# Linear attention into a rational feed-forward layer on one core: weights built with 16-bit low bits, their low parts made by a transfer that adds

## The chip, the cores and the metric

The kernel runs on one core of one Trainium2 chip. The metric is the device time of one execution in microseconds (us); lower is better. Shown are the median of three runs and one profiled execution. The engines are TensorE (PE in the profile, PEld its weight loads), VectorE (DVE), ScalarE (ACT), GpSimd (POOL) and the queue that issues most transfers (SP).

## The reference, cut to what matters

```
kv  = einsum('bhsd,bhse->bhde', k, v)        # 8 batches, 8 heads, 576 positions, 64 wide
out = einsum('bhsd,bhde->bhse', q, kv)
out = out / sqrt(mean(out*out, -1) + 1e-6) * g_norm
x   = out.transpose(0, 2, 1, 3).reshape(4608, 512)
h   = x @ w_in                               # w_in 512 x 2048, 64-bit floats
P   = a0 + a1*h + a2*h^2 + a3*h^3
Q   = 1 + |b0|*|h| + |b1|*h^2
y   = (P / (Q + 1e-6)) @ w_out               # w_out 2048 x 512, 64-bit floats
```

The two weight matrices come as 64-bit floats. The kernel makes 32-bit floats of them on the chip.

## The kernel before, in words

**Tiles and slots.** The 4608 tokens are nine tiles `t` of 512. The 2048 hidden columns are sixteen chunks `c` of 128. A pair `(t, c)` is a slot; slots have a running number `i`, so 0 to 15 are the first tile (t = 0), 16 to 31 the second (t = 1), and so on. One Python loop over the slots sets the order of work on each engine, which is kept as written. In slot `i`, TensorE computes `gemm2` of slot `i-2` (h's function times `w_out`, added up in four `acc` tiles of PSUM), then matmuls of attention for the tile after this one, then `gemm1` of slot `i+1` (x times `w_in` into one of two `h` tiles). ScalarE and VectorE compute the rational function of slot `i` between them (`ew_a`, `ew_b`, `ew_c`: ACT lines L458, L459, L461, L471, L472, DVE lines L460, L462, L468, L476, L478, L484).

**Split and unsplit.** The first tile multiplies 32-bit floats as they are (lines L444 and L507; the profile counts two MATMUL records for each). The other tiles write each operand as a high part rounded to `float32r` and a low part, the difference, and multiply low by high, high by low and high by high: three matmuls (L448 to L450, L511 to L513). The function's result is split in `ew_d` (`gh` on ACT L494, `gl` on DVE L495). `unsplit(t, c)` says where `gemm2` uses whole floats: the first tile, and the last four chunks of the second (`LATE = 12`), because the low parts of those weights are made later.

**Weights.** A unit is a pair of chunks of `w_in` ("wi") or `w_out` ("wo"), 128 x 1024 words of 64 bits; there are sixteen. `fetch_w` loads one through SP. To make 32-bit floats, `signs` (GpSimd, L224) multiplies the high words by zero, which leaves their signs; `conv_a` (ACT, L192, two passes) scales the low and the high words in place; `conv_c` (DVE, for each half of a unit) shifts the high words by 3 and ors them into the signs (L229), then adds the low words (L230). The first two units go another way (`conv_b1`, L208; `conv_b2`, L212 and L216), ahead of the loop. The table `schedule` gives for each unit the slot of its load, of its `conv_a`, and of its split. `signs` of a unit starts, by a dependency added by hand, after DVE's L460 of the slot whose ACT does `conv_a`.

**Splitting weights.** `split_w` casts the unit to its high part on ACT (L247) and, at the end of the slot's DVE work, subtracts on DVE (L254, 128 x 1024). Low parts go where an earlier unit's whole floats stood. The last unit is copied away first (`w_last`).

Of the kernel before, what the change touches and what calls it, by code (L numbers as in the profile page):

```python
# [23 lines left out]
def linear_attention_then_rational_ffn(  # L24
# [93 lines left out]
    def f32(t):  # L118
# [6 lines left out]
        ("wi", 0): (None, None, 13),  # L125
        ("wi", 2): (None, None, 15),
        ("wo", 0): (None, None, 16),
        ("wi", 4): (-1, 0, 17),
        ("wo", 2): (-1, 1, 18),
        ("wi", 6): (-1, 2, 19),  # L130
        ("wo", 4): (-1, 3, 19),
        ("wi", 8): (0, 4, 20),
        ("wo", 6): (0, 5, 21),
        ("wi", 10): (1, 6, 21),
        ("wo", 8): (2, 7, 23),
        ("wi", 12): (3, 8, 23),
        ("wo", 10): (4, 9, 24),
        ("wi", 14): (5, 10, 26),
        ("wo", 12): (6, 11, 33),
# [83 lines left out]
    def signs(u, part):  # L223
        return POOL.tensor_scalar(room(u)[:, part], f32(words(u, part)[1]), 0.0, None, ALU.mult)  # L224

    def conv_c(u, part):
        low, high = words(u, part)
        w = ups[u].bitcast(I32)[:, part]
        DVE.scalar_tensor_tensor(w, high, 3, w, ALU.logical_shift_left, ALU.bitwise_or)  # L229
        DVE.tensor_tensor(w, w, low, ALU.add)  # L230
# [6 lines left out]
    def split_w(u):  # L237
# [11 lines left out]
        def rest():  # L249
# [4 lines left out]
            DVE.tensor_tensor(wl, w, f32(wh), ALU.subtract)  # L254
# [376 lines left out]
    conv_b1(u1, two)  # L631

# [4 lines left out]
    for i, (t, c) in enumerate(slots[:-1]):  # L637
        q_made = ew_a(t, c, ph)
        for u in at_slot(1, i):

            tc.add_manual_dep(signs(u, both).ins, q_made.ins.name, beside, reason="signs beside h")
        if i:
            ew_d(*slots[i - 1])
        rest = {0: [], 1: [], 2: []}
        convs = [lambda u=u, j=j: (conv_b2 if u == u1 else conv_c)(u, (one, two)[j]) for u, j in made.get(i, [])]
# [27 lines left out]
        if c == NF - 2 and t < NTILE - 1:  # L673
# [51 lines left out]
```

## Time and profile before

| | |
|---|---|
| median of 3 runs | 906.61 us (906.58 to 906.76) |
| profiled execution, span from first to last instruction | 904.8 us |
| between that span and the median | 1.8 us |
| PE busy | 895.7 us, 99% |
| DVE busy | 792.6 us, 88% |
| ACT busy | 689.8 us, 76% |
| POOL busy | 50.5 us, 6% |
| DMA, mean over the span | 73 GB/s |

The page gives no time for the profiled execution other than its span, so the sum below is made against 904.8 us and carried over to the median. A busy PE is not a PE at its peak: the matmuls' ends are modelled, and a start-to-start distance says more than a duration. Rows of the timeline give the start in us, the duration in us, engine, line, operation and tiles; in square brackets the idle time ahead of it and what ended that. Rows of windows give the stretch, its length, and for each engine the busy time and the number of instructions, then the granted clock, the share of DMA and GB/s.

### The profile page before, as it was taken

What the parts mean: (1) busy time and instruction counts of PE and PEld (TensorE: products, weight loads), DVE (VectorE), ACT (ScalarE), POOL (GpSimd) and SP (SyncE); (2) the same over time, 40 slices, a digit from 0 to 9 for tenths busy, and PEclk for the clock granted to TensorE, in tenths of its full rate; (3) what the DMA queues carried; (4) which work ended last, traced back from release to release, by engine and by line L of the source; (5) the groups of instructions that cost most, each with busy time, mean ns of one, the idle gap of its engine ahead of it and who ended that gap; (6) DMA issues with size and microseconds to landing.
All of it is one profiled execution on the core that took longest, in us unless ns stands there. A gap on an engine that the chain in (4) does not pass through costs nothing.

```text
span 904.8 us, 11685 instructions
## 1 busy us (share of the span) xinstructions
PE 895.7 (99%) x4278; PEld 676.7 (75%) x4278; DVE 792.6 (88%) x1250; ACT 689.8 (76%) x1167; POOL 50.5 (6%) x63
## 2 busy tenths in 40 slices
PE   8999999999999999999999999999999999999998
PEld 6444446778678788878887888788878887888886
DVE  3998999999897898889887998799778988898887
ACT  5898867888687778777877686778777787777665
POOL 3444310000000000000000000000000000000000
PEclk9999999999999999999999999999999999999999
DMA  9964002211122203210311122121301020201001
GB/s 367 359 239 146 25 24 96 75 42 47 42 91 79 48 1 129 82 35 14 119 58 35 48 88 82 41 49 41 117 24 48 0 70 13 48 0 47 1 1 47
DMA packets 23961, 65.89 MB, mean 73 GB/s; under 512 B 2336, under 2 KB 2336, under 8 KB 23904
## 3 DMA queue, kind: packets, MB, share of 16 engines
q1 hardware_dynamic: 23328, 64.10, 21.6%
q10 hardware_dynamic: 576, 1.05, 0.3%
q8 instruction: 33, 0.54, 0.3%
q14 instruction: 24, 0.20, 0.1%
HBM read 55.58 MB, written 9.57 MB: 72 GB/s over the span
## 4 chain that ended last, share of the span: by engine, by line
PE 88%; DVE 7%; ACT 2%; DMA 1%; issue 1%; SPq 0%; DVEq 0%; ACTq 0%
PE h L448 13%; PE acc L511 12%; PE h L450 12%; PE h L449 12%; PE acc L513 12%; PE acc L512 12%; PE acc L507 5%; PE h L444 4%; PE kvp L331 2%; DMA first<-in_first_dram 1%; DVE q L460 1%; PE ms L375 1%; PE op L362 1%; PE op L363 1%; DVE u L462 1%
## 5 line engine op out<-in xcount | busy, mean ns | idle before, releaser
L448 PE MATMUL h<-x,parts 128*128 128x512 f32 (+1 forms) x516 | 205.7, 399 | 0.0
L450 PE MATMUL h<-x,parts 128*128 128x512 f32 (+1 forms) x516 | 200.5, 389 | 0.0
L458 ACT ACTIVATE d<-h 128x512 f32<-128x512 f32 x143 | 85.8, 600 | 149.2 <-PE h L450 145.8
L512 PE MATMUL acc<-wol,gh 128*128 128x512 f32 x492 | 191.5, 389 | 0.0
L460 DVE SCALAR_TENSOR_TENSOR q<-d,b1abs,q 128x512 f32<-128x512 f32 x143 | 107.1, 749 | 81.1 <-ACT q L459 80.9
L449 PE MATMUL h<-x,wil 128*128 128x512 f32 (+1 forms) x452 | 175.5, 388 | 0.0
L511 PE MATMUL acc<-parts,gl 128*128 128x512 f32 x440 | 171.9, 391 | 0.7 <-ACT ob L519 0.4
L513 PE MATMUL acc<-parts,gh 128*128 128x512 f32 x440 | 171.2, 389 | 0.0
L471 ACT ACTIVATE d<-q,bias 128x512 f32<-128x512 f32 x143 | 105.5, 738 | 28.5 <-DVE q L460 27.5
L448 PEld LDWEIGHTS h<-x,parts 128*128 128x128 f32 x516 | 96.9, 188 | 26.4 <-DVE gl L495 5.0
L461 ACT ACTIVATE u<-h,na 128x512 f32<-128x512 f32 x143 | 112.7, 788 | 0.0
L450 PEld LDWEIGHTS h<-x,parts 128*128 128x128 f32 x516 | 96.9, 188 | 20.6
L472 ACT ACTIVATE d<-d,bias 128x512 f32<-128x512 f32 x143 | 103.6, 724 | 4.7
L478 DVE SCALAR_TENSOR_TENSOR u<-u,na,d 128x512 f32<-128x512 f32 x143 | 106.8, 747 | 0.0
L468 DVE SCALAR_TENSOR_TENSOR u<-u,na,h 128x512 f32<-128x512 f32 x143 | 106.0, 741 | 0.7
L512 PEld LDWEIGHTS acc<-wol,gh 128*128 128x128 f32 x492 | 92.4, 188 | 18.9
L476 DVE SCALAR_TENSOR_TENSOR q<-q,d 128x512 f32<-128x512 f32 x143 | 98.3, 687 | 0.8 <-ACT d L472 0.8
L462 DVE TENSOR_TENSOR u<-u,h 128x512 f32<-128x512 f32 x143 | 97.9, 685 | 0.8
L459 ACT ACTIVATE q<-h,abg 128x512 f32<-128x512 f32 x143 | 98.1, 686 | 0.0
L511 PEld LDWEIGHTS acc<-parts,gl 128*128 128x128 f32 x440 | 82.6, 188 | 19.7 <-DVE gl L495 1.9
L449 PEld LDWEIGHTS h<-x,wil 128*128 128x128 f32 x452 | 85.0, 188 | 16.2 <-issue 0.2
L513 PEld LDWEIGHTS acc<-parts,gh 128*128 128x128 f32 x440 | 82.6, 188 | 17.3
(142 smaller groups left out, 1120.3 us busy)
## 6 DMA issues: line engine op xcount, KB each, us to landing
kvm<-in_kv_dram SPq DMA_DIRECT2D x28, 640.0 KB
raw_wo<-in_w_out_dram SPq DMA_DIRECT2D x8, 1024.0 KB
qr<-in_qT_dram SPq DMA_DIRECT2D x32, 256.0 KB
out_dram<-ob SPq DMA_DIRECT2D x16, 512.0 KB
rb<-rd SPq DMA_DIRECT2D x28, 256.0 KB
raw_wi<-in_w_in_dram SPq DMA_DIRECT2D x6, 1024.0 KB
first<-in_first_dram SPq DMA_DIRECT2D x4, 640.0 KB
raw_wi<-in_w_in_dram SPq DMA_DIRECT2D x4, 512.0 KB
```

Source lines behind the costliest of these rows:

```text
L448: PE.matmul(ph, wh, xl, start=(kc == 0), stop=False)
L449: PE.matmul(ph, wl, xh, start=False, stop=False)
L450: PE.matmul(ph, wh, xh, start=False, stop=(kc == NPAIR - 1))
L460: q_made = DVE.scalar_tensor_tensor(q, d, b1abs, q, ALU.mult, ALU.add)
L461: ACT.activation(u, ph, AF.Identity, bias=na[:, 2:3], scale=na[:, 3:4])
L462: DVE.tensor_tensor(u, u, ph, ALU.mult)
L468: DVE.scalar_tensor_tensor(u, u, na[:, 1:2], ph, ALU.add, ALU.mult)
L471: ACT.activation(d, q, AF.Ln, bias=bias[:, 2:3], scale=QSC)
L478: DVE.scalar_tensor_tensor(u, u, na[:, 0:1], d, ALU.add, ALU.mult)
L511: PE.matmul(o, gl[:, ss], wh, start=(c == 0), stop=False)
L512: PE.matmul(o, gh[:, ss], wl, start=False, stop=False)
L513: PE.matmul(o, gh[:, ss], wh, start=False, stop=(c == NF - 1))
```

## The change

Four edits go together; lines from L222 on move by up to 10 in the new file (L460 becomes L464, L254's place becomes L257 and L258).

1. **Low bits as 16-bit words.** `conv_a` scales the high words first, then writes the scaled low words as 16-bit integers straight into the low half of the words that `signs` wrote. `conv_shift` (DVE, once for a unit, 128 x 1024) shifts the high words in place. `conv_c` is then one addition for each half. `signs` of a unit comes one slot earlier; those of the first two such units stand ahead of the loop, without the dependency on L460.
2. **Low parts by transfer.** In `split_w`, GpSimd writes the negated high part into the low part's place (L257) and then issues a transfer that adds the unit to it (L258). DVE no longer subtracts.
3. **Second tile split throughout.** `unsplit` holds for the first tile alone.
4. **Earlier splits.** The third column of `schedule` runs from slot 11 to 30; it ran from 13 to 35.

```diff
-        ("wi", 0): (None, None, 13),
+        ("wi", 0): (None, None, 11),
...
-        ("wo", 14): (7, 12, 35),
+        ("wo", 14): (7, 12, 30),
     }
-    LATE = 12
...
     def unsplit(t, c):
-        return t == 0 or t == 1 and c >= LATE
+        return t == 0
...
     def conv_a(u, part=both, engine="S"):
         low, high = words(u, part)
-        scale(engine, low, low.bitcast(U32), 2.0**-29)
         scale(engine, f32(high), f32(high), 2.0**-112)
+        to = low if u in units[:2] else ups[u].bitcast(U16).rearrange("p (f w) -> p f w", w=2)[:, part, 0]
+        scale(engine, to, low.bitcast(U32), 2.0**-29)
...
+    def conv_shift(u):
+        high = words(u, both)[1]
+        DVE.tensor_scalar(high, high, 3, None, ALU.logical_shift_left)
+
     def conv_c(u, part):
-        low, high = words(u, part)
         w = ups[u].bitcast(I32)[:, part]
-        DVE.scalar_tensor_tensor(w, high, 3, w, ALU.logical_shift_left, ALU.bitwise_or)
-        DVE.tensor_tensor(w, w, low, ALU.add)
+        DVE.tensor_tensor(w, w, words(u, part)[1], ALU.add)
...
-            DVE.tensor_tensor(wl, w, f32(wh), ALU.subtract)
+            POOL.tensor_scalar(wl, f32(wh), -1.0, None, ALU.mult)
+            POOL.dma_start(wl, w, accum_op=ALU.add)
...
-    signs(u2, both)
+    signs(u2)
     conv_a(u1, one)
     conv_a(u1, two)
+    for u in at_slot(1, 0):
+        signs(u)
     conv_a(u2)
...
     conv_b1(u1, two)
+    conv_shift(u2)
...
-        for u in at_slot(1, i):
-            tc.add_manual_dep(signs(u, both).ins, q_made.ins.name, beside, reason="signs beside h")
+        for u in at_slot(1, i + 1):
+            tc.add_manual_dep(signs(u).ins, q_made.ins.name, beside, reason="signs beside h")
...
         for u in at_slot(1, i):
             conv_a(u)
+            shifts.append(u)
...
+        rest[2] += [lambda u=u: conv_shift(u) for u in shifts]
```

How the order of instructions moves, at two places. In these rows `wow_297` is the unit wo 0 (the third made), `raw_wi_245` the raw words of wi 4 (the fourth), `wiw_317` and `wiw_319` the unit wi 2. The first place is the start, on GpSimd, from the last of its setup on; before:

```order
L115 MEMSET kvh_130 128x128
L116 MEMSET kvl_136 128x128
L224 TENSOR_SCALAR wow_297<-raw_wo_155 128x1024 [waits DMAHW4_49]
L224 TENSOR_SCALAR wiw_335<-raw_wi_245 128x1024 [waits DMAHW5_49,DVE_49]
L224 TENSOR_SCALAR wow_367<-raw_wo_251 128x1024 [waits DMAHW0_49,DVE_49]
```

and in the changed kernel:

```order
L116 MEMSET kvh_130 128x128
L117 MEMSET kvl_136 128x128
L225 TENSOR_SCALAR wow_297<-raw_wo_155 128x1024 [waits DMAHW4_49]
L225 TENSOR_SCALAR wiw_303<-raw_wi_245 128x1024 [waits DMAHW5_49]
L225 TENSOR_SCALAR wow_338<-raw_wo_251 128x1024 [waits DMAHW0_49,DVE_49]
```

The signs of wi 4 no longer wait for DVE; they follow those of wo 0 as soon as their words have landed.

On DVE at the same place, from the last work ahead of the loop to the first slot's function, before:

```order
L208 TENSOR_SCALAR wiw_317<-raw_wi_152 128x512
L212 SCALAR_TENSOR_TENSOR wiw_317<-raw_wi_152,wiw_317 128x512
L216 ISA wiw_317<-raw_wi_152,wiw_317 128x1024
L208 TENSOR_SCALAR wiw_317<-raw_wi_152 128x512
L460 SCALAR_TENSOR_TENSOR q_0_328<-d_0_327,b1abs,q_0_328 128x512
L462 TENSOR_TENSOR u_0_329<-u_0_329,h_0_322 128x512
L468 SCALAR_TENSOR_TENSOR u_0_329<-u_0_329,na,h_0_322 128x512
L229 SCALAR_TENSOR_TENSOR wow_297<-raw_wo_155,wow_297 128x512
L230 ISA wow_297<-raw_wo_155,wow_297 128x1024
```

and in the changed kernel:

```order
L209 TENSOR_SCALAR wiw_319<-raw_wi_152 128x512
L213 SCALAR_TENSOR_TENSOR wiw_319<-raw_wi_152,wiw_319 128x512
L217 ISA wiw_319<-raw_wi_152,wiw_319 128x1024
L209 TENSOR_SCALAR wiw_319<-raw_wi_152 128x512
L229 TENSOR_SCALAR raw_wo_155<-raw_wo_155 128x1024
L464 SCALAR_TENSOR_TENSOR q_0_331<-d_0_330,b1abs,q_0_331 128x512
L466 TENSOR_TENSOR u_0_332<-u_0_332,h_0_325 128x512
L472 SCALAR_TENSOR_TENSOR u_0_332<-u_0_332,na,h_0_325 128x512
L233 ISA wow_297<-raw_wo_155,wow_297 128x1024
```

The shift of wo 0 (L229 of the new file) stands ahead of the first slot's function, and one conversion step less stands behind it.

The second place is the second tile, DVE's rows of slot 17 (`gl_0` belongs to slot 16), before:

```order
L460 SCALAR_TENSOR_TENSOR q_1_1063<-d_1_1062,b1abs,q_1_1063 128x512
L462 TENSOR_TENSOR u_1_1064<-u_1_1064,h_1_1041 128x512
L495 TENSOR_TENSOR gl_0_1071<-u_0_1007,gh_0_1070 128x512
L468 SCALAR_TENSOR_TENSOR u_1_1064<-u_1_1064,na,h_1_1041 128x512
L476 SCALAR_TENSOR_TENSOR q_1_1063<-q_1_1063,d_1_1062 128x512
L478 SCALAR_TENSOR_TENSOR u_1_1064<-u_1_1064,na,d_1_1062 128x512
L484 SCALAR_TENSOR_TENSOR u_1_1064<-q_1_1063,u_1_1064 128x512
L254 TENSOR_TENSOR wil_1118<-wiw_335,parts_1089 128x1024
```

and in the changed kernel:

```order
L464 SCALAR_TENSOR_TENSOR q_1_1075<-d_1_1074,b1abs,q_1_1075 128x512
L466 TENSOR_TENSOR u_1_1076<-u_1_1076,h_1_1055 128x512
L499 TENSOR_TENSOR gl_0_1083<-u_0_1022,gh_0_1082 128x512
L472 SCALAR_TENSOR_TENSOR u_1_1076<-u_1_1076,na,h_1_1055 128x512
L480 SCALAR_TENSOR_TENSOR q_1_1075<-q_1_1075,d_1_1074 128x512
L482 SCALAR_TENSOR_TENSOR u_1_1076<-u_1_1076,na,d_1_1074 128x512
L488 SCALAR_TENSOR_TENSOR u_1_1076<-q_1_1075,u_1_1076 128x512
```

The subtraction that closed the slot is gone, here and in every slot that had one.

On GpSimd in the changed kernel, from the last signs (slot 11) to the low parts of wi 0, wi 2 and wo 0 (`DMASW` counts the landings of GpSimd's own transfers):

```order
L225 TENSOR_SCALAR wow_823<-raw_wo_679 128x1024 [waits DMAHW1_49,DVE_49,PE_49]
L257 TENSOR_SCALAR parts_847<-parts_847 128x1024 [waits Activation_49]
L258 DMA parts_847<-wiw_279 128x1024 [waits Pool_49]
L257 TENSOR_SCALAR wil_894<-parts_880 128x1024 [waits DMASW0_49,Activation_49]
L258 DMA wil_894<-wiw_319 128x1024 [waits Pool_49]
L257 TENSOR_SCALAR wol_931<-parts_880 128x1024 [waits DMASW1_49,Activation_49]
L258 DMA wol_931<-wow_297 128x1024 [waits Pool_49]
```

GpSimd, which had nothing behind the signs, now has a negation and a transfer for each unit, and each negation waits for the landing of the transfer before.

More of the change, by code (lines that the diff above doesn't have):

```diff
@@ L12 @@
 U32 = mybir.dt.uint32
+U16 = mybir.dt.uint16
 AF = mybir.ActivationFunctionType
@@ L124, in linear_attention_then_rational_ffn @@
     schedule = {
-        ("wi", 0): (None, None, 13),
[L126 to L139, printed above, removed]
-        ("wo", 14): (7, 12, 35),
+        ("wi", 0): (None, None, 11),
+        ("wi", 2): (None, None, 12),
+        ("wo", 0): (None, None, 13),
+        ("wi", 4): (-1, 0, 13),
+        ("wo", 2): (-1, 1, 14),
+        ("wi", 6): (-1, 2, 14),
+        ("wo", 4): (-1, 3, 15),
+        ("wi", 8): (0, 4, 15),
+        ("wo", 6): (0, 5, 17),
+        ("wi", 10): (1, 6, 18),
+        ("wo", 8): (2, 7, 19),
+        ("wi", 12): (3, 8, 21),
+        ("wo", 10): (4, 9, 22),
+        ("wi", 14): (5, 10, 23),
+        ("wo", 12): (6, 11, 25),
+        ("wo", 14): (7, 12, 30),
     }
-    LATE = 12
     units = list(schedule)
@@ L220, in conv_b2, with signs @@
         conv_add(u, part)
-    def signs(u, part):
-        return POOL.tensor_scalar(room(u)[:, part], f32(words(u, part)[1]), 0.0, None, ALU.mult)
+    def signs(u):
+        return POOL.tensor_scalar(room(u), f32(words(u, both)[1]), 0.0, None, ALU.mult)
+    def conv_shift(u):
+        high = words(u, both)[1]
+        DVE.tensor_scalar(high, high, 3, None, ALU.logical_shift_left)
     def conv_c(u, part):
-        low, high = words(u, part)
         w = ups[u].bitcast(I32)[:, part]
-        DVE.scalar_tensor_tensor(w, high, 3, w, ALU.logical_shift_left, ALU.bitwise_or)
-        DVE.tensor_tensor(w, w, low, ALU.add)
+        DVE.tensor_tensor(w, w, words(u, part)[1], ALU.add)
     def gpart(k, j):
@@ L644, in linear_attention_then_rational_ffn @@
         rest = {0: [], 1: [], 2: []}
+        shifts = []
         convs = [lambda u=u, j=j: (conv_b2 if u == u1 else conv_c)(u, (one, two)[j]) for u, j in made.get(i, [])]
```

## The prediction

> **What bounds the kernel now.** I read the page's busy times and its chain of waits first, then windows over single slots of TensorE, then who waited for whom in the slow ones, then the timeline at the start.
>
> ```profile
> PE 895.7 (99%) x4278; PEld 676.7 (75%) x4278; DVE 792.6 (88%) x1250; ACT 689.8 (76%) x1167; POOL 50.5 (6%) x63
> PE 88%; DVE 7%; ACT 2%; DMA 1%; issue 1%; SPq 0%; DVEq 0%; ACTq 0%
> ```
>
> TensorE bounds it: 88% of the chain is its own work, and DVE has 7%. So an edit pays where it shortens TensorE's work, or where TensorE waits. The first window below is the first tile. The four others are cut at the first L448 of a slot, so that each is a whole number of slots.
>
> ```profile
> 22.40:134.20 111.80, 111.79 (x345) 50.28 (x345) 106.01 (x162) 91.47 (x138) 43.77 (x22) 1.00 0.43 161
> 148.77:190.78 42.01, 40.43 (x223) 30.75 (x223) 39.53 (x60) 36.54 (x63) 0.00 (x0) 1.00 0.28 91
> 251.18:289.10 37.92, 37.92 (x224) 31.12 (x223) 32.88 (x54) 30.59 (x57) 0.00 (x0) 1.00 0.32 101
> 224.79:251.18 26.39, 26.39 (x107) 16.43 (x106) 23.59 (x38) 18.41 (x31) 0.00 (x0) 1.00 0.11 36
> 322.99:346.42 23.43, 23.43 (x123) 19.32 (x122) 23.31 (x40) 18.89 (x33) 0.00 (x0) 1.00 0.13 40
> ```
>
> In the first tile TensorE is busy without a break (111.79 of 111.80). The second window is slots 18 to 23, in the second tile; the third the same six slots one tile later: the same matmuls, 42.01 us against 37.92, and DVE busy for 39.53 of the 42.01 (its column is the third of busy times). The fourth is slots 30 to 33, where `gemm2` of the last four chunks of the second tile is unsplit; the fifth is the same one tile later, split: 26.39 against 23.43.
>
> What TensorE and ScalarE waited for in slots 15 to 25 (total, times, longest):
>
> ```profile
> PEld op L361 <- DVE ql L346: 2.2, 4, 0.7
> PEld acc L511 <- DVE gl L495: 1.7, 4, 0.6
> PEld kvp L331 <- ACT xf L367: 1.6, 3, 0.8
> ACT d L471 <- DVE q L460: 9.2, 7, 2.3
> ```
>
> DVE is late there, and ACT waits for it. One cause is the splitting of weights, whose rows from 148.77 to 190.78 are:
>
> ```profile
> L254 DVE TENSOR_TENSOR wil<-wiw,parts 128x1024 fp32r<-128x1024 f32 x4 | 4.9, 1221 | 0.6 <-ACT parts L247 0.5
> L254 DVE TENSOR_TENSOR wol<-wow,parts 128x1024 fp32r<-128x1024 f32 x4 | 4.9, 1219 | 0.1
> ```
>
> **The change part by part.** *Second tile split.* Matmuls end to end in both forms, and attention's matmuls of the two tiles:
>
> ```profile
> 127.72 3.60 PE L444 MATMUL h<-x,wiw 128*128 128x512 f32 x8
> 131.15 3.60 PE L507 MATMUL acc<-wow,g 128*128 128x512 f32 x8
> 176.11 0.33 PE L361 MATMUL op<-ql,kvh 128*128 128x128 f32 x1 [0.29 <-DVE ql L346]
> 177.08 0.39 PE L448 MATMUL h<-x,parts 128*128 128x512 f32 x1
> 285.60 0.39 PE L511 MATMUL acc<-parts,gl 128*128 128x512 f32 x1
> 288.32 0.25 PE L361 MATMUL op<-ql,kvh 128*128 128x192 f32 x1
> 289.10 0.39 PE L448 MATMUL h<-x,parts 128*128 128x512 f32 x1
> ```
>
> Four whole-float matmuls (eight records) take 131.15 - 127.72 = 3.43 us, the twelve split ones 288.32 - 285.60 = 2.72. Four slots change: 4 x 0.71 = 2.84 us. The windows give 26.39 - 23.43 = 2.96. I take 2.9. In exchange ACT casts four times and DVE subtracts four times for `gh` and `gl`, as in the window at 322.99, where DVE is busy for 23.31 of 23.43 us and TensorE does not wait. That is the cover, and it is thin; if it fails, the subtractions come to 4 x 0.7 = 2.8 us at most.
>
> *Subtractions off DVE.* Slots 18 to 23 need 37.92 us of TensorE plus what attention's other piece sizes add: 177.08 - 176.11 = 0.97 us against 289.10 - 288.32 = 0.78, in three slots, 0.57. So 42.01 - 37.92 - 0.57 = 3.5 us are waits. Without the eight L254, DVE has 39.53 - 9.8 = 29.7 us of work for 38.5, and ACT's 36.54 fits too, with fewer weight casts there. Nothing is left that is late, so I take all of 3.5; the bounds are 0 and 3.5. The subtractions, or-steps and shifts of the first tile are worth nothing by themselves: TensorE runs there without waiting from slot 2 on, so what DVE saves only shortens the backlog that it carries into slot 16.
>
> *The 16-bit words.* For a unit, two or-steps and two additions become one shift and two additions. ACT's two passes stay. Neither ends a chain after slot 2, except through GpSimd, below. ACT's write of 16-bit words has no row; the 32-bit form took 1.17 us for a pass at 107.61, and I take the same. If it cost half as much again, 0.6 us in a slot, ACT's idle time in the first tile would cover it: it is busy for 91.47 of 111.80 us.
>
> *The start.* Here both DVE and ACT are on the path:
>
> ```profile
> 21.25 2.83 POOL L224 TENSOR_SCALAR wow<-raw_wo 128x1024 f32<-128x1024 f32 x1 [14.48 <-DMA raw_wo<-in_w_out_dram]
> 24.11 1.18 ACT L192 ACTIVATE raw_wo<-raw_wo 128x1024 f32<-128x1024 f32 x1 [1.50 <-POOL wow L224]
> 24.24 0.42 DVE L208 TENSOR_SCALAR wiw<-raw_wi 128x512 int32<-128x512 int32 x1
> 26.03 0.42 DVE L208 TENSOR_SCALAR wiw<-raw_wi 128x512 int32<-128x512 int32 x1
> 26.13 0.60 ACT L458 ACTIVATE d<-h 128x512 f32<-128x512 f32 x1 [0.84 <-PE h L444]
> 27.34 0.75 DVE L460 SCALAR_TENSOR_TENSOR q<-d,b1abs,q 128x512 f32<-128x512 f32 x1 [0.90 <-ACT q L459]
> 29.54 0.30 PEld L444 LDWEIGHTS h<-x,wiw 128*128 128x128 f32 x2 [0.84 <-DVE u L468]
> ```
>
> ACT did the low pass of wo 0 while it waited for the signs; now the high pass, which needs them, comes first, and the low pass behind it: 24.11 + 1.18 + 1.1 = 26.4, so L458 starts at 26.3 and not at 26.13. DVE's new shift stands at 26.4 and, at L208's 0.42 us for half as many words, takes 0.7 to 0.84; DVE idled 0.90 us there. The third `gemm1` waits for this slot's L468 (29.54), so the delay counts: +0.2 us.
>
> *GpSimd's splits.* A negation of 128 x 1024 has no row. Its nearest rows are the signs, the same operation on as many words with a stride, and a memset of that size:
>
> ```profile
> 0.86 0.95 POOL L72 MEMSET kvf<- 128x1024 f32 x1
> 106.28 2.87 POOL L224 TENSOR_SCALAR wow<-raw_wo 128x1024 f32<-128x1024 f32 x1 [3.80 <-DVE q L460]
> 107.49 0.69 DVE L229 SCALAR_TENSOR_TENSOR wow<-raw_wo,wow 128x512 int32<-128x512 int32 x1
> 107.61 1.17 ACT L192 ACTIVATE raw_wo<-raw_wo 128x1024 int32<-128x1024 uint32 x1
> 227.51 2.74 PE L507 MATMUL acc<-wow,g 128*128 128x512 f32 x6
> 305.93 1.15 SPq L392 DMA_DIRECT2D rd<-r  x4
> 307.52 1.92 SPq L406 DMA_DIRECT2D rb<-rd  x3
> ```
>
> So 0.95 to 2.87 us; I take 2.87, the nearer row. A transfer that adds has no row either. The four small stores at 305.93 have landed when the load at 307.52 is issued, so latency is under a microsecond. The start moves 366 GB/s over 22.4 us:
>
> ```profile
> 0.00:22.40 22.40, 19.30 (x159) 13.36 (x159) 7.24 (x14) 12.42 (x26) 6.76 (x42) 1.00 0.93 366
> ```
>
> 512 KB is 1.4 us at that rate; with the addend and the target read and the sum written as three such passes, 4.3. So 2.1 to 5 us, and I take 3.5, the middle. One unit is then 6.4 us, with ends at 3.1 and 7.9. Negations wait for the transfer before, so units follow one another. The first can start when ACT has cast wi 0 in slot 11, at about 110.8 (107.61 plus two passes and a cast). wo 12, the fifteenth, is first needed by slot 30's `gemm2`, at 227.51 - 3.5 = 224.0: (224.0 - 110.8) / 15 = 7.5 us for each. At 6.4 all are in time and cost nothing. wo 14 alone is tight. ACT's work in a slot of that place is 18.89 / 4 = 4.7 us, so its cast in slot 30 ends near 224.0 + 4.7 = 228.7; slot 32's `gemm2` comes two slots of 2 x 2.72 later, at 234.9. That leaves 6.2 us for 6.4, and DVE's copy of the unit stands ahead of the cast: +0.4, between 0 and 1.7.
>
> *The sum:* -2.9 - 3.5 + 0.2 + 0.4 = -5.8 us. The profiled span of 904.8 becomes 899.0, and the median, 1.8 above it, 900.8.
>
> **A rule against the change.** Beside GpSimd's signs at 106.28, DVE's L229, with two operands in SBUF, took 0.69 us as always. The Trainium skill, "SBUF — State Buffer", section "Who interferes with whom", says that such an instruction contends with a GpSimd instruction that reads SBUF, and that a DVE instruction in a two-port mode and a GpSimd instruction fully block each other, whoever issues first. The trace does not agree with the first half; no run here shows the second. By the first half sixteen negations would hold DVE up for as long as they last, and the sum would be lost; I go by the row.
>
> **The rivals.** *DVE blocked by GpSimd's signs.* L208 takes 0.42 us for 512 words where L229 takes 0.69, so it runs in another way, and the shift is of its kind; in the old kernel no such instruction ran beside GpSimd. Now the signs of wi 4 follow at 24.1 (its 1 MB lands about 2.9 us after wo 0's at 366 GB/s, near 24.1), and last to 27.0, across both L208 and the shift. If they shut these out, L208 begins at 27.0 and L460 at 29.85: 2.5 us late, all of it passed on by the wait at 29.54. In slots 11 and 12 the negations of wi 0 and wi 2 would meet the last two shifts, 2.9 us each, partly absorbed. That gives 900.8 + 2.3 = 903.1, up to 905. The second half of the page's rule is this rival. For it: nothing in the trace denies it. Against: L229 was not held up.
>
> *The transfers are the bound (slower).* If one negation with its transfer takes over 7.5 us, TensorE waits for 15 times the excess: 8.0 us for a unit loses 7.5 and gives 908.3, 8.4 gives 914. It decides against the change from 7.9 us on, the upper end above. For it: neither part has a row of its own. Against: both would have to lie at their upper ends.
>
> *DVE was not what was late.* If ACT, with its casts drawn forward to two in each of slots 13 to 15, is late in its place, the 3.5 shrink to about 1: 903.3. ACT's waits of 9.2 us for DVE speak against it.
>
> **How the numbers follow.** My forecast has 0.48, DVE blocked 0.30, transfers as the bound 0.11, ACT late 0.11. The forecast's own range is 899.9 (no cost for wo 14 and the start) to 902.0. The whole range, 899.8 to 905.0, leaves out the transfers as the bound and a little above each case. A measurement here tells 0.2%, 1.8 us, from no change: under 904.8 is faster. That holds for the forecast, nearly all of ACT late, and most of DVE blocked: 0.82. Within 0.2%: 0.09, from the tails and a chain just over 7.5 us. Slower: 0.09.
>
> **What would show it.** Right: no L511 or L361 of slots 18 to 23 waits for DVE; slots 30 to 33 take 23.4 us; the third `gemm1` starts within 0.3 us of 29.54; no TensorE wait is ended by a GpSimd transfer but for a short one at wo 14. Wrong: L208 at the start is drawn out or late by 2 us or more; L453 or L516 wait for transfers from slot 24 on; L516's first wait in slot 32 exceeds 2 us; a negation is longer than 3 us.

## The result, and the profile after

| | before | after |
|---|---|---|
| median of the runs on one chip | 906.64 us (906.58 to 906.76) | 915.38 us (912.84 to 916.09) |
| ratio | | 1.0091 (95% interval 1.0078 to 1.0104) |
| span of the profiled execution | 904.8 us | 914.2 us |

The kernel became slower, by 0.9%. The forecast was 900.8 us, between 899.8 and 905.0. The profiled execution is the slowest of the four, 916.09 us. The page of the changed kernel, its busy times and its chain of waits:

```profile
PE 894.6 (98%) x4294; PEld 682.2 (75%) x4294; DVE 774.3 (85%) x1224; ACT 692.4 (76%) x1171; POOL 111.4 (12%) x95
PE 83%; DMA 8%; POOL 4%; DVE 3%; issue 1%; ACT 1%; SPq 0%; POOLq 0%; ACTq 0%; DVEq 0%
```

DVE went from 7% of the chain to 3%, as meant; but DMA went from 1% to 8% and GpSimd came in with 4%. Windows of the changed kernel (us; then busy time and count of PE, PEld, DVE, ACT, POOL; granted clock, DMA share, GB/s), cut at the first matmul of a slot's `gemm1` except for the last two:

```profile
149.39:187.54 38.15, 38.15 (x223) 31.34 (x223) 32.02 (x51) 33.49 (x60) 15.02 (x8) 1.00 0.64 162
199.67:254.52 54.85, 43.06 (x189) 33.95 (x187) 41.20 (x62) 32.75 (x52) 20.12 (x11) 0.94 0.39 77
310.92:349.83 38.91, 38.91 (x190) 32.01 (x188) 37.84 (x61) 30.54 (x50) 0.00 (x0) 1.00 0.12 28
222.00:226.00 4.00, 3.94 (x11) 3.21 (x12) 2.20 (x3) 0.00 (x0) 3.59 (x2) 0.61 0.00 0
238.00:244.00 6.00, 5.41 (x17) 4.34 (x18) 2.00 (x4) 1.50 (x2) 3.13 (x2) 0.72 0.01 3
```

The first row is slots 18 to 23: 38.15 us, where the kernel before took 42.01, and TensorE never idle. The second is slots 26 to 32, the third the same seven slots one tile later: 54.85 - 38.91 = 15.9 us are lost there. The last two rows lie inside the second. Behind each of its two long waits TensorE's clock was granted at 0.61 for 4 us and at 0.72 for 6 us, about 4 x 0.39 + 6 x 0.28 = 3.2 us of the 15.9. What TensorE waited for between 195 and 250 us (total, times, longest):

```profile
PE acc L516 <- DMA wol<-wow: 6.6, 2, 4.9
PE acc L516 <- ACT d L476: 3.9, 1, 3.9
PE h L453 <- DMA wil<-wiw: 1.2, 1, 1.2
```

L516 is the second matmul of a split `gemm2`, the first to read a weight's low part; L453 is the same in `gemm1`. Two rows name the transfers. The middle one is put down to ACT's L476, which writes nothing that L516 reads and happened to end at the same time: it is L516 of slot 30's `gemm2`, at 238.59, which needs wo 12, and wo 12's transfer, issued at 233.91, lands 4.6 us later, at 238.5. Between the two kernels' traces the account is, by the start of each slot:

| stretch | before | after | difference |
|---|---|---|---|
| to the third `gemm1` | 29.54 | 30.17 | +0.63 |
| from there to slot 18 | 119.23 | 119.22 | 0 |
| slots 18 to 23 | 42.01 | 38.15 | -3.86 |
| slots 24 and 25 | 12.15 | 12.13 | 0 |
| slots 26 to 33 | 48.25 | 61.21 | +12.96 |

That is +9.7 us, of which the end of the kernel gives 0.3 back. The +12.96 are the 15.9 us lost, waits and lower clock together, less 3.0 for the split.

The chain behind it, GpSimd's timeline in slots 17 to 19 (start, duration, instruction, idle time before it and what ended that), and two of SP's loads at that place:

```profile
144.08 2.76 POOL L257 TENSOR_SCALAR wol<-parts 128x1024 fp32r<-128x1024 f32 x1 [3.85 <-DMA wil<-wiw]
147.13 0.89 POOL L258 DMA_DIRECT2D wol<-wow  x1 [0.30 <-POOL wol L257]
151.87 2.77 POOL L257 TENSOR_SCALAR wil<-parts 128x1024 fp32r<-128x1024 f32 x1 [3.85 <-DMA wol<-wow]
154.93 0.89 POOL L258 DMA_DIRECT2D wil<-wiw  x1 [0.30 <-POOL wil L257]
161.24 2.77 POOL L257 TENSOR_SCALAR wol<-parts 128x1024 fp32r<-128x1024 f32 x1 [5.41 <-ACT gh L498]
...
155.80 0.35 SPq L315 DMA_DIRECT2D kvm<-in_kv_dram  x1
159.57 0.35 SPq L319 DMA_DIRECT2D qr<-in_qT_dram  x1
```

A unit is a negation of 2.76 us, 0.30 until the transfer is issued, 0.89 for issuing it, and 3.85 until it has landed and the next negation starts: 7.8 us. The next unit waits because its negation writes into the room that this transfer still reads. Beside the loads of K, V and Q the landing takes 1.6 us longer (5.41 for 3.85), and that unit takes 9.4 us. (The row puts this wait down to ACT's L498; `e11_noload` below shows that it was the transfer.) From the first negation at 111.26 to the fifteenth at 230.46 there are fourteen steps of 8.5 us each, against the 7.5 us that the schedule allows. Issue to landing, shortest, median and longest of the sixteen transfers:

```profile
DMA to landing us min/median/max: 4.5/4.6/6.6
```

The start, on GpSimd and DVE of the changed kernel:

```profile
24.18 2.83 POOL L225 TENSOR_SCALAR wiw<-raw_wi 128x1024 f32<-128x1024 f32 x1
24.32 1.25 DVE L209 TENSOR_SCALAR wiw<-raw_wi 128x512 int32<-128x512 int32 x1
27.04 0.42 DVE L209 TENSOR_SCALAR wiw<-raw_wi 128x512 int32<-128x512 int32 x1
28.00 0.73 DVE L464 SCALAR_TENSOR_TENSOR q<-d,b1abs,q 128x512 f32<-128x512 f32 x1
```

L209, 0.42 us without GpSimd beside it, took 1.25 us beside the signs of wi 4, and L464 starts at 28.00 where L460 started at 27.34.

### The profile page after: what moved, and what is told of

Its sections match the earlier page's. It is cut to its first block, busy times and chain, and to the rows that moved or that the text cites. A ratio compares the mean times of both kernels' runs of the same rounds, so it can differ in the third digit from the quotient of the medians.

```text
span 914.2 us, 11768 instructions
## 1 busy us (share of the span) xinstructions
PE 894.6 (98%) x4294; PEld 682.2 (75%) x4294; DVE 774.3 (85%) x1224; ACT 692.4 (76%) x1171; POOL 111.4 (12%) x95
## 4 chain that ended last, share of the span: by engine, by line
PE 83%; DMA 8%; POOL 4%; DVE 3%; issue 1%; ACT 1%; SPq 0%; POOLq 0%; ACTq 0%; DVEq 0%
PE h L452 12%; PE acc L516 11%; PE acc L517 11%; PE acc L515 11%; PE h L454 11%; PE h L453 11%; PE h L448 5%; PE acc L511 4%; DMA wil<-wiw 4%; DMA wol<-wow 3%; PE kvp L335 2%; POOL wil L257 2%; POOL wol L257 2%; DMA first<-in_first_dram 1%; PE ms L379 1%
## 5 line engine op out<-in xcount | busy, mean ns | idle before, releaser
L516 PE MATMUL acc<-wol,gh 128*128 128x512 f32 x508 | 199.2, 392 | 10.5 <-DMA wol<-wow 6.6
L464 DVE SCALAR_TENSOR_TENSOR q<-d,b1abs,q 128x512 f32<-128x512 f32 x143 | 108.6, 759 | 104.5 <-ACT q L463 104.4
L453 PE MATMUL h<-x,wil 128*128 128x512 f32 (+1 forms) x452 | 175.6, 388 | 1.2 <-DMA wil<-wiw 1.2
L517 PE MATMUL acc<-parts,gh 128*128 128x512 f32 x448 | 175.5, 392 | 0.0
L515 PE MATMUL acc<-parts,gl 128*128 128x512 f32 x448 | 175.4, 391 | 0.0
L516 PEld LDWEIGHTS acc<-wol,gh 128*128 128x128 f32 x508 | 96.1, 189 | 31.7 <-issue 5.3
L482 DVE SCALAR_TENSOR_TENSOR u<-u,na,d 128x512 f32<-128x512 f32 x143 | 109.0, 762 | 0.0
L476 ACT ACTIVATE d<-d,bias 128x512 f32<-128x512 f32 x143 | 103.6, 724 | 4.7
L480 DVE SCALAR_TENSOR_TENSOR q<-q,d 128x512 f32<-128x512 f32 x143 | 98.4, 688 | 0.2 <-ACT d L476 0.2
L453 PEld LDWEIGHTS h<-x,wil 128*128 128x128 f32 x452 | 85.0, 188 | 17.6 <-DMA wil<-wiw 1.7
L515 PEld LDWEIGHTS acc<-parts,gl 128*128 128x128 f32 x448 | 84.8, 189 | 17.8
L517 PEld LDWEIGHTS acc<-parts,gh 128*128 128x128 f32 x448 | 84.9, 189 | 17.6
L463 ACT ACTIVATE q<-h,abg 128x512 f32<-128x512 f32 x143 | 97.9, 685 | 0.0
```

What stands on the lines that cost most here:

```text
L453: PE.matmul(ph, wl, xh, start=False, stop=False)
L464: q_made = DVE.scalar_tensor_tensor(q, d, b1abs, q, ALU.mult, ALU.add)
L476: ACT.activation(d, d, AF.Exp, bias=bias[:, 3:4], scale=-1.0)
L482: DVE.scalar_tensor_tensor(u, u, na[:, 0:1], d, ALU.add, ALU.mult)
L515: PE.matmul(o, gl[:, ss], wh, start=(c == 0), stop=False)
L516: PE.matmul(o, gh[:, ss], wl, start=False, stop=False)
```

## The experiments

Each was timed beside the kernel before on the same chip (906.6 to 906.7 us in each set). Slot times are from one `gemm1`'s first matmul to the next one's.

### How long a unit is

**e10_copy**: the transfers copy and don't add.

```diff
-            POOL.dma_start(wl, w, accum_op=ALU.add)
+            POOL.dma_start(wl, w.bitcast(F32R))
```

> The changed kernel with the transfers copying instead of adding (left out: the subtraction, the low part becomes the weight itself); negations, order, rooms and waits as in the changed kernel. It measures what adding costs in a transfer of 512 KB, 4.7 us from issue to landing in the changed kernel. Theory A (the addend, the target and the sum are three passes, as the prediction's middle of 3.5 us supposed, so a copy is two of them): a copy lands after about 3.3 us, the unit falls from 8.1 to 6.7 us, under 7.5, and the waits in slots 26 to 32 go: 901 to 903 us. Theory B (issue and landing have a fixed part of some 3 us and the adding itself costs little): the copy lands after 4.2 us or more, the unit stays at 7.4 to 7.8 us, and TensorE still waits for 3 us or more: 904 to 912 us.

Measured: 902.13 us, ratio 0.9950 (0.9934 to 0.9966). Its transfers, two units on GpSimd, and slots 26 to 32:

```profile
DMA to landing us min/median/max: 2.9/3.0/6.1
145.20 2.76 POOL L257 TENSOR_SCALAR wil<-parts 128x1024 fp32r<-128x1024 f32 x1 [3.12 <-DMA wol<-wow]
148.25 0.57 POOL L258 DMA_DIRECT2D wil<-wiw  x1 [0.30 <-POOL wil L257]
151.35 3.29 POOL L257 TENSOR_SCALAR wol<-parts 128x1024 fp32r<-128x1024 f32 x1 [2.53 <-DMA wil<-wiw]
199.51:240.82 41.31, 40.12 (x189) 31.70 (x188) 39.42 (x61) 32.61 (x52) 10.18 (x6) 1.00 0.24 65
```

A copy of 512 KB lands after 3.0 us in the median, an addition after 4.6: adding costs 1.6 us, 0.3 of it in the issue. A unit from 145.20 to 151.35 takes 6.15 us, and of the 15.9 us lost 41.31 - 38.91 = 2.4 are left, 2.1 of them in slot 32, where TensorE waits for DVE and for no transfer. Theory A held. The negations, the order and the rooms are the same here, so the length of the transfer by itself turns a gain of 4.5 us into a loss of 8.7.

**e6_memset**: the other part of the unit made shorter.

```diff
-            POOL.tensor_scalar(wl, f32(wh), -1.0, None, ALU.mult)
+            POOL.memset(f32(wl), 0.0)
```

> The changed kernel with each negation replaced by a memset of zeros of the same room, so the transfer adds to zero and the low part is wrong by the high part: left out is the subtraction. It shortens the unit by about 1.9 us (0.95 for 2.85) and leaves the transfer as it is. Theory (the unit is negation 2.85 + handing over 0.25 + issue to landing 4.7, in series): cadence 0.95 + 0.25 + 4.7 = 5.9 us, under 7.5, waits of TensorE in slots 26 to 32 gone but for up to 2 us at wo 14, 899 to 903 us. Rival (transfers take as long as they do because they queue behind each other or behind loads, so a shorter instruction ahead of them frees nothing): cadence stays near 7.5 to 8 us and 5 us or more of waits stay, 908 to 914 us.

Measured: 901.56 us, ratio 0.9944 (0.9928 to 0.9961). The memset takes 0.95 us, the transfers 4.7 in the median (4.6 in the changed kernel), and no wait of TensorE for a transfer is left. The parts are in series, and it is enough to shorten one of them.

**e11_noload**: some loads beside the transfers are left out.

```diff
     def fetch_kvq(t, p):
+        if t == 2 and p or (t, p) == (3, 0):
+            kvq[t, p] = kvq_last[-1]
+            return
...
         kvq[t, p] = m, q
+        kvq_last.append((m, q))
```

> The changed kernel without four of the loads of K, V and Q that fall into tile 1's slots 16 to 24 (left out: pairs 1 to 3 of tile 2 and pair 0 of tile 3 are computed from pair 0's data again); everything else as in the changed kernel. There four of the transfers took 6.2 to 6.6 us to land and not 4.6, three of them issued beside those loads and one beside the broadcasts at 207 us, and a unit took 8.5 us in the mean where the short ones take 7.8. Theory (the loads share the DMA engines with the adding transfers, which doubles the excess over 7.5 us): the three land after 4.6 to 4.8 us, the chain ends about 5 us sooner and TensorE waits 9 to 12 us and not 15.9: 908 to 912 us. Rival (the long ones come from something else, such as the engines that GpSimd waits for): they stay long, 914 to 916 us.

Measured: 910.50 us, ratio 1.0044 (1.0028 to 1.0061). The unit that took 9.4 us beside a load, and slots 26 to 32:

```profile
154.83 0.89 POOL L258 DMA_DIRECT2D wil<-wiw  x1 [0.30 <-POOL wil L257]
159.55 3.12 POOL L257 TENSOR_SCALAR wol<-parts 128x1024 fp32r<-128x1024 f32 x1 [3.83 <-DMA wil<-wiw]
199.61:248.48 48.87, 41.74 (x190) 33.39 (x188) 40.56 (x62) 33.06 (x52) 18.89 (x10) 0.93 0.38 78
```

The negation behind that issue waits 3.83 us and not 5.41; the loss is 48.87 - 38.91 = 10.0 us and not 15.9. So the loads that shared the DMA engines with the transfers made about 6 of the 15.9 us. The one beside the broadcasts, which stayed, still took 6.2. But of the three that should have become short, one, issued at 171.10, still took 5.9 us with no load beside it; the trace has one packet of the instruction queue in that stretch and nothing else, and what it does to a transfer was not tried.

### When it starts

**e2_early**: the same units in slots 8, 9, 10 and so on, one for a slot to slot 18 and then nearly so, wo 14 in slot 30.

```diff
-        ("wi", 0): (None, None, 11),
+        ("wi", 0): (None, None, 8),
...
-        ("wo", 6): (0, 5, 17),
+        ("wo", 6): (0, 5, 16),
...
-        ("wo", 12): (6, 11, 25),
+        ("wo", 12): (6, 11, 24),
```

> The changed kernel with one thing moved: the units' splits are scheduled from slot 8 on, one for a slot, instead of from slot 11 on; wo 14 stays in slot 30. Same negations, same adding transfers. Theory (a unit takes about 8 us, against the 7.5 us that the time from the first cast to slot 30 allows): started some 20 us sooner, 15 units have 134 us, 8.9 us for each, so the cadence stays at 7.8 to 8.7 us and the waits for wo 12 and before go; only wo 14 may still make TensorE wait up to 5 us. 899 to 904 us. Rival 1 (waits come from the places late in the schedule, wi 14 and wo 14 and DVE's copy): little changes, 910 to 915 us. Rival 2 (negations beside DVE cost time by contention): the first tile gets longer, by 0.8 us for each of 8 negations, up to 6 us.

Measured: 904.96 us, ratio 0.9979 (0.9970 to 0.9988), a little above what was expected. Slots 16 to 20 and 26 to 32, and TensorE's waits from 195 to 250 us:

```profile
134.84:170.60 35.76, 34.48 (x186) 24.28 (x184) 31.86 (x49) 32.42 (x56) 14.18 (x9) 1.00 0.58 140
201.87:243.62 41.75, 40.04 (x189) 31.77 (x187) 40.31 (x63) 32.19 (x52) 11.18 (x6) 1.00 0.31 64
PE acc L515 <- DVE gl L499: 0.8, 1, 0.8
PE acc L516 <- DMA wol<-w_last: 0.7, 1, 0.7
```

Only wo 14's transfer still ends a wait, for 0.7 us. What is left is mostly DVE: 35.76 us against 33.58 in the changed kernel for slots 16 to 20, and 2.8 us in slot 32, with that wait. The first tile did not get longer, so rival 2's place was wrong; its cause may be at work behind the first tile, which no run here shows by itself.

### Who does the subtraction

**e1_dve_sub**: DVE subtracts again, the rest as in the changed kernel.

```diff
-            POOL.tensor_scalar(wl, f32(wh), -1.0, None, ALU.mult)
-            POOL.dma_start(wl, w, accum_op=ALU.add)
+            DVE.tensor_tensor(wl, w, f32(wh), ALU.subtract)
```

> The changed kernel, but the low parts of the weights are subtracted by DVE again (one instruction of about 1.2 us for a unit, as in the kernel before); 16-bit words, the split second tile and the schedule stay. Theory (the chain of negations and adding transfers is what is late, 15.9 us of TensorE waits in slots 26 to 32): the waits go, span 914.2 - 15.9 = 898.3, plus up to 2 us where DVE is late again, so 900 to 903 us. Rival 1 (the schedule drawn forward or the thin cover in slots 30 to 33 is what costs, whoever subtracts): waits of 5 us or more stay in slots 26 to 32, 906 to 915 us. Rival 2 (DVE slowed by GpSimd's readers is what costs): also fast here, but it then must stay slow in the two kernels in which GpSimd keeps its own long instructions.

Measured: 908.41 us, ratio 1.0022 (1.0013 to 1.0031). Slots 16 to 18, four microseconds inside them, and slots 30 to 33:

```profile
134.66:162.53 27.87, 24.24 (x112) 16.19 (x111) 24.88 (x36) 21.56 (x37) 0.00 (x0) 0.88 0.21 71
154.00:158.00 4.00, 4.00 (x11) 3.18 (x10) 3.58 (x6) 3.97 (x8) 0.00 (x0) 0.50 0.38 140
228.27:254.42 26.15, 24.12 (x123) 19.22 (x122) 25.02 (x42) 19.64 (x34) 0.00 (x0) 1.00 0.12 36
```

The waits for transfers are gone, but the expectation missed. Slots 16 to 18 take 27.87 us for 20.87 in the changed kernel. DVE, with eight subtractions drawn forward into slots 11 to 15, comes late out of the first tile, and TensorE waits 3.6 us for it (27.87 - 24.24), 3.2 of them in one wait that ends at 152.44. The other 3.3 us are TensorE's clock behind that wait, granted at 0.50 from 154 to 158 and at 0.88 over the whole stretch (27.87 x 0.12 = 3.3). So rival 1 was right in kind and wrong in place: without the transfers, the schedule drawn forward makes DVE late instead, which costs 7.0 us there, and 2.7 us are lost in slot 32.

**e4_pool_sub**: GpSimd subtracts by itself (`POOL.tensor_tensor(wl, w, f32(wh), ALU.subtract)`, no transfer).

> The changed kernel with GpSimd subtracting by itself (one instruction with two operands, low part = weight minus high part) and no transfers. Theory (the landing of each transfer, 4.7 us of a unit's 8, is what makes the chain late): if GpSimd's subtraction takes under 7 us for 128 x 1024, units keep up, the waits go and the time is 899 to 903 us. Rival 2 (GpSimd's reads beside DVE cost time): DVE's two-operand instructions that start beside it are drawn out from 0.7 to 1.5 us, and with GpSimd busy for longer than 2.8 us a unit, DVE is late in slots 18 to 23: 904 to 912 us.

Measured: 916.75 us, ratio 1.0110 (1.0095 to 1.0125), above both ranges. GpSimd and DVE at one place of `e4_pool_sub`, and then a negation of the changed kernel with the DVE instruction that starts beside it:

```profile
148.11 2.88 POOL L257 TENSOR_TENSOR wol<-wow,parts 128x1024 fp32r<-128x1024 f32 x1 [5.19 <-ACT parts L250]
148.80 2.74 DVE L487 SCALAR_TENSOR_TENSOR g<-q,u 128x512 f32<-128x512 f32 x1
151.07 2.72 POOL L257 TENSOR_TENSOR wil<-wiw,parts 128x1024 fp32r<-128x1024 f32 x1
151.46 2.87 DVE L463 SCALAR_TENSOR_TENSOR q<-d,b1abs,q 128x512 f32<-128x512 f32 x1
...
119.50 3.06 POOL L257 TENSOR_SCALAR wil<-parts 128x1024 fp32r<-128x1024 f32 x1 [3.85 <-ACT q L463]
119.85 1.53 DVE L464 SCALAR_TENSOR_TENSOR q<-d,b1abs,q 128x512 f32<-128x512 f32 x1
```

GpSimd's subtraction is as short as its negation, 2.7 us. But DVE's instruction of 0.69 us that starts beside it takes 2.74, until GpSimd has ended; about a dozen of these, mostly +2.1 us each, make DVE late in slots 15 to 19. Beside a negation, with one operand, an instruction that starts near its beginning takes up to 1.55 us instead of 0.75; ten such cost DVE 6.8 us in the changed kernel. Beside `e6_memset`'s memsets none was drawn out. The Trainium skill, "SBUF — State Buffer", section "Who interferes with whom", says that a DVE instruction with two SBUF operands contends with a GpSimd instruction that reads SBUF and not with one that only writes; the memsets, the subtractions and the negations agree, but a negation holds DVE for at most 0.9 us of its 2.8.

**e7_act_neg**: `e2_early` with the negation on ACT (`ACT.activation(wl, f32(wh), AF.Copy, scale=-1.0)`).

> The early schedule of e2_early, with the negation on ACT (one more ACT pass of about 1.05 us for a unit) instead of GpSimd; GpSimd only issues the adding transfers. Theory (what was left in e2_early, 1.3 us in slot 16, 0.7 in slot 19 and 2.8 in slot 32, is DVE late because each of GpSimd's negations draws out one DVE instruction by 0.8 us; a unit is 1.05 + 0.3 + 4.7 = 6 us): DVE's instructions keep their length, and the span falls from 903.3 to 899 to 900.5, 900.5 to 902 us. Rival (ACT, busy for 24.6 of 26.3 us in slots 18 to 21 of e2_early, becomes late with three more passes of 1.05 us, or stands still for a transfer): 1.5 to 4 us of waits for ACT in slots 16 to 23, 903 to 906 us.

Measured: 910.22 us, ratio 1.0037 (1.0024 to 1.0050), above the rival's range too. Slots 16 to 20, and a wait of ACT there (total, times, longest):

```profile
134.86:175.63 40.77, 35.43 (x186) 24.04 (x185) 29.65 (x48) 36.16 (x60) 4.30 (x5) 1.00 0.59 139
ACT wol L257 <- DMA wil<-wiw: 3.5, 2, 2.1
```

DVE is lighter (29.65 us, none of its instructions drawn out), and the stretch is still longer: ACT is busy for 36.16 us, more than the 33.58 that these slots take when nothing is late. On top of that its negations, which write into the room that the transfer before reads, stood for 4.0 us in ACT's queue until that had landed (3.5 by the row, and 0.5 at 142.74). Together that is 40.2 of the 40.77 us: ACT had become the bound, and the rival was right in both of its reasons.

**e12_alt**: every second unit subtracted by DVE, the others as in the changed kernel.

```diff
+            if i % 2:
+                DVE.tensor_tensor(wl, w, f32(wh), ALU.subtract)
+                return
             POOL.tensor_scalar(wl, f32(wh), -1.0, None, ALU.mult)
```

> The changed kernel with every second unit (wi 2, wi 4, wi 6, wi 8, wi 10, wi 12, wi 14 and wo 14) subtracted by DVE and the others by GpSimd's negation and the adding transfer. Theory (eight units of 8.5 us have twice the time, so the chain is not late; DVE pays 1.2 us for each of its eight units and is held for 0.8 us by each of the eight negations): no wait of TensorE for a transfer, 1 to 3 us of waits for DVE in slots 16 to 18 where e1_dve_sub had 7, and about 2.7 us in slot 32: 902 to 905.5 us. Rival (DVE is as late as in e1_dve_sub, since being held costs it nearly as much as subtracting): 906 to 908.5 us.

Measured: 921.92 us, ratio 1.0170 (1.0155 to 1.0185): the worst of all, and both theories missed it. DVE's longest wait, and the sum of such waits from 120 to 250 us:

```profile
158.68 1.23 DVE L258 TENSOR_TENSOR wil<-wiw,parts 128x1024 fp32r<-128x1024 f32 x1 [6.12 <-DMA wol<-wow]
DVE wil L258 <- DMA wol<-wow: 17.5, 5, 6.1
```

The transfers are no longer the pace of the chain, but DVE's subtraction writes into the room that the transfer before it reads, and so it stands in DVE's queue until that has landed, with the slot's function behind it. In the changed kernel the same wait stood on GpSimd, where nothing was queued behind it but the next unit.

### The other parts alone

**e8_words**: the kernel before with the 16-bit words only (the first item of the change). **e9_split**: the kernel before with the second tile split throughout, and

```diff
-        ("wo", 12): (6, 11, 33),
-        ("wo", 14): (7, 12, 35),
+        ("wo", 12): (6, 11, 28),
+        ("wo", 14): (7, 12, 30),
```

> The kernel before with only the 16-bit words (signs of wi 4 at the start, ACT's low pass into the sign words, shift and add on DVE); schedule, unsplit chunks of tile 2 and DVE's subtractions as before. Theory (at the start +0.6 us, as in the changed kernel; a unit costs DVE about 0.7 us less in the first tile, which shortens the backlog that ends in slots 18 to 23, where 3.5 us are waits): +0.6 and -1 to -3.5, so 903.7 to 906.2 us. Rival (DVE's savings in the first tile are worth nothing, since TensorE never waits there): +0.6, 907.2 us.

> The kernel before with only the whole of tile 2 split: the splits of wo 12 and wo 14 come in slots 28 and 30 instead of 33 and 35, DVE's subtractions and the words as before. Theory (four slots lose 0.71 us each, and DVE's cover in slots 30 to 33 is thin): -2.9, with up to 2.7 us of waits for DVE in slots 30 to 32, so 903.7 to 906.5 us. Rival (the cover fails: DVE, busy for 22.4 of 22.9 us there, gets four gl and two subtractions more, 5.2 us, and one copy): same or slower, 906.5 to 909 us.

Measured: `e8_words` 904.79 us, ratio 0.9978 (0.9969 to 0.9987); `e9_split` 908.68 us, ratio 1.0022 (1.0013 to 1.0032). Slots 18 to 23 of `e8_words`, and slots 30 to 33 of `e9_split`:

```profile
149.32:189.31 39.99, 39.50 (x223) 30.96 (x223) 37.55 (x57) 35.70 (x62) 0.00 (x0) 1.00 0.28 90
225.00:253.35 28.35, 25.22 (x123) 18.91 (x122) 27.22 (x44) 20.51 (x35) 0.00 (x0) 1.00 0.11 33
```

The words alone take 2.0 of the 3.5 us of waits away (39.99 for 42.01), with DVE's subtractions still in these slots: what DVE saves in the first tile is worth something after all, as a shorter backlog. The split alone costs 28.35 - 26.39 = 2.0 us instead of saving 2.9: DVE is busy for 27.22 of the 28.35 us, and the casts and subtractions of wo 14 meet the splitting of the next tile's x there.

**e5_signs0**: the changed kernel with the signs of wi 4 behind slot 0's q.

```diff
-    for u in at_slot(1, 0):
-        signs(u)
     conv_a(u2)
...
-        for u in at_slot(1, i + 1):
+        for u in (at_slot(1, 0) if i == 0 else []) + at_slot(1, i + 1):
```

> The changed kernel with the signs of wi 4 behind slot 0's q, as before, and not at the start. Theory (the third gemm1 is 0.63 us late, at 30.17 for 29.54, because the signs of wi 4 draw out DVE's L209 from 0.42 to 1.25 us): L209 takes 0.42 us again and the third gemm1 starts at 29.6 to 29.8; the rest as in the changed kernel, with the waits of slots 26 to 32, so 914.5 to 916 us. Rival (ACT's low pass behind the high pass is what is late): L209 is short and the third gemm1 stays at 30.0 or later.

Measured: 914.54 us, one run. DVE at the start:

```profile
24.44 0.42 DVE L209 TENSOR_SCALAR wiw<-raw_wi 128x512 int32<-128x512 int32 x1
26.33 0.42 DVE L209 TENSOR_SCALAR wiw<-raw_wi 128x512 int32<-128x512 int32 x1
27.57 0.75 DVE L464 SCALAR_TENSOR_TENSOR q<-d,b1abs,q 128x512 f32<-128x512 f32 x1 [0.21 <-ACT q L463]
```

L209 is short again, and the third `gemm1` starts at 29.76, which is 7.16 us after the first one, nearly as before (29.54 - 22.40 = 7.14; 7.69 in the changed kernel). So GpSimd's signs were most of the delay in this pair of runs. They were not all of it: in the three kernels below, which have the same start and a short L209 too, the distance is 7.25, 7.37 and 7.49 us, and there L464 waits 0.30 to 0.55 us for ACT's L463, behind ACT's pass of 1.35 us that writes the 16-bit words.

### Three versions put together from these

**b2_words** is `e8_words` with the start of `e5_signs0`. **b3_dve** is `b2_words` with `LATE = 14` and wo 12 in slot 28. **b1_mix** keeps negations and transfers, in slots 8 to 13 and 16 to 26, with chunks 14 and 15 unsplit, wo 14 in slot 35, and the start of `e5_signs0`:

```diff
-        return t == 0
+        return t == 0 or t == 1 and c >= 14
```

> The kernel before with the 16-bit words alone (e8_words, 904.8 us), and the signs of wi 4 behind slot 0's q as they were, so that L209 runs without GpSimd beside it. Theory: 0.4 to 0.55 us less than e8_words, as the third gemm1 of e5_signs0 showed (29.76 for 30.17): 904.2 to 904.5 us. Rival: the start is caught up by DVE's backlog and nothing is gained, 904.8 us.

> b2_words with chunks 12 and 13 of tile 2 split as well (wo 12 split in slot 28, wo 14 in slot 35 as before), DVE subtracting. Theory (a split chunk saves TensorE 0.71 us; e9_split lost its gain in slots 30 to 32, where wo 14's copy, cast and subtraction met DVE's x splits, and that work is not there now): -1.4, 902.8 to 903.5 us. Rival (DVE is late in slots 28 to 32 with the two gl more and wo 12's subtraction): no gain or a loss, 904 to 905.5 us.

> The changed kernel with the negations and adding transfers kept, but scheduled in slots 8 to 13 and 16 to 26 (none in slots 14 and 15, where DVE splits x), chunks 14 and 15 of tile 2 unsplit with wo 14 in slot 35, and the signs of wi 4 behind slot 0's q. Theory (e2_early's 903.3 us of span had 1.3 in slot 16, 0.7 in slot 19, 2.8 in slot 32 and 0.5 at the start too much; unsplit chunks cost 1.4): 899.4 us of span and 901.2 us, 900.3 to 902.5. Rival (eight negations in the first tile, each holding DVE for 0.8 us, leave a backlog wherever they stand): waits for DVE of 1 to 3 us in slots 16 to 19, 902.5 to 905 us.

Measured: `b2_words` 904.48 us, 0.9976 (0.9966 to 0.9986); `b3_dve` 904.02, 0.9972 (0.9961 to 0.9982); `b1_mix` 902.41, 0.9953 (0.9938 to 0.9968). In `b2_words` the third `gemm1` came 7.37 us after the first, 7.61 in `e8_words`, and the two ratios cannot be told apart. `b3_dve` got a third of its 1.4 us, as its rival said. `b1_mix` is faster than both kernels; its slots 16 to 20 and 30 to 33:

```profile
134.57:168.99 34.42, 33.98 (x186) 24.42 (x184) 30.54 (x50) 29.76 (x52) 13.88 (x8) 1.00 0.55 140
222.11:247.07 24.96, 24.96 (x115) 17.87 (x114) 24.46 (x41) 19.23 (x33) 0.00 (x0) 1.00 0.12 37
```

0.85 us of waits are left in slot 16 (34.42 for 33.58); slots 30 to 33 have none. The same transfers as in the changed kernel, begun three slots sooner, with two chunks left unsplit and a clear place for DVE, give 902.4 us and not 915.4.

## Why the prediction was wrong, by its own steps

**The step that failed is the price of the adding transfer.** The prediction took 3.5 us, the middle between 2.1 and 5; measured from issue to landing it was 4.6 in the median and up to 6.6. The price was sized as three passes over the bytes with a latency under a microsecond, read from SP's small stores; a plain copy of the same 512 KB already takes 3.0 us. The Trainium skill, "DMA: Bandwidth & Descriptors", section "Anatomy of one DMA — SWDGE (gpsimd) path", gives a fixed part of about 2.0 us and the bytes at 436 GB/s beside it; an estimate by that is 3.2 us for a copy. The measured copy, 3.0 us, agrees. Two things stood in no term: the 0.30 us between negation and issue, and the loads of K, V and Q, which run in the same slots. So the unit was 7.8 us undisturbed and 8.5 in the mean, and not 6.4; even the upper end, 7.9, was too low. The price alone (2.87 + 4.6) would have brought the unit to the limit of 7.5 us. At 7.8 us for each unit the loss would have been 15 x 0.3 = 4.5 us; the four transfers that landed after 6.1 to 6.6 us, three beside those loads and one beside the broadcasts, added another 7, and negations longer than 2.76 us most of the rest.

**The negation** was taken at 2.87 us and took 2.76 to 3.28. That is near; six of the sixteen took over 3 us, which the prediction had named as a sign of being wrong, but without the transfer's price they would not have mattered.

**The threshold and the rival.** (224.0 - 110.8) / 15 = 7.5 us held, and so did the rival's formula: 15 x (8.5 - 7.5) = 15 us, measured 15.9. (The formula has no clock in it; the lower clock behind the last wait, 6 x 0.28 = 1.7 us, lies on top of it.) What was wrong was its chance of 0.11: the forecast's 6.4 and the limit's 7.5 lay 1.1 us apart, less than the uncertainty of the transfer alone. `e10_copy`, with a unit of 6.2 us undisturbed and 6.8 in the mean, is the world that was forecast, and its 902.13 us lie 1.3 above the 900.8.

**Subtractions off DVE, -3.5**: -3.86 measured, right in size. The 0.57 us set aside for other piece sizes were too much, since the 0.97 us were read behind a wait; undisturbed the piece is 162.12 - 161.26 = 0.86 us in the changed kernel. The reason was half right: `e8_words` has 2.0 us of it with the subtractions still on DVE. That savings in the first tile are worth nothing by themselves was wrong, in both directions: with the schedule drawn forward and DVE subtracting, `e1_dve_sub` loses 7 us behind the first tile, half of it waits for DVE and half the clock behind them.

**The split, -2.9**: TensorE's part is right (3.0 in the account above), visible because DVE could catch up while TensorE waited. The cover called thin does fail: `e9_split` loses 4.9 us there (28.35 for 23.43), more than the 2.8 us put as the most. The bound left out the splitting of wo 14, which came into the same slots: in `b3_dve`, with wo 14 in slot 35 and two chunks unsplit, these slots take 25.82 us, 1.0 above the 23.43 + 2 x 0.71 that TensorE needs. In the kernels that don't wait for earlier transfers 1.5 to 2.8 us stay in slot 32 (`e6_memset`, `e10_copy`, `e2_early`, the last with 0.7 for wo 14's transfer), where wo 14 was given 0.4.

**The start, +0.2**: +0.63, of which 0.08 is the first `gemm1`, at 22.48 for 22.40. The term itself was about right: with the signs away, 0.02 to 0.35 us are left. The rest is the first rival in a milder form: the signs held L209 back by 0.83 us, not until they ended at 27.0, and the shift not at all. The Trainium skill, "SBUF — State Buffer", section "Who interferes with whom", has a full block for the whole instruction where DVE runs in a two-port mode. The trace does not show one: L209 took 1.25 us beside signs of 2.83; whether it runs in such a mode no run shows.

**The rule against the change**, on instructions with two operands: set aside on the row of the signs, it was half true of the negations, 6.8 us of DVE's time. That row did not even hold for all signs: in `e2_early` three DVE instructions of 0.69 us took 2.2 us where signs ran beside them, L480 at 94.21 for one. The 6.8 us stayed beside other work in the changed kernel; in `e2_early` such time is the likely part of what slots 16 to 20 lost, which is argued, not shown.

## What to carry to other kernels

A chain whose units wait for each other is as long as the sum of its parts, with the hand-over, the issue, the landing and the transfers that run beside it; compare that sum with the time allowed per unit, and where the margin is smaller than the uncertainty of one unseen part, give the bad case the larger chance. If it is close, start the chain sooner before making it shorter: three slots were worth 10 us here. And keep a wait for a landing on an engine that has nothing else queued: the same wait cost more in DVE's queue (`e12_alt`) than the whole chain had, and in ACT's (`e7_act_neg`) it held ACT for 4.0 us.

## What the hardware showed that was not expected

- A GpSimd transfer of 512 KB inside SBUF took 3.0 us from issue to landing as a copy and 4.6 us when adding; its issue took 0.57 and 0.89 us; beside loads from DRAM an adding one took up to 6.6 us, and 7.3 in `e2_early`.
- A DVE instruction of 0.7 us took up to 1.55 us beside the beginning of a GpSimd negation (one operand), 2.2 us beside some of GpSimd's signs (one operand too), mostly 2.7 to 2.9 us beside a subtraction (two operands), and its usual time beside a memset.
- Behind waits of 4 to 5 us TensorE's clock was granted at 0.61 and 0.72 over the next 4 to 6 us, which made a fifth of the loss; behind a wait of 3.2 us in `e1_dve_sub` it was 0.50 for 4 us.
